# Batch 0's loads split by chunk and moved between queues, constant set-up moved to VectorE, and two early table-loading activations added, in a fused scan and MLP kernel

## The chip, the core and the metric

The kernel runs on one core of a Trainium2 chip. The core has five instruction streams that run side by side and wait for each other through semaphores: TensorE (PE, with its weight loads PEld shown apart), VectorE (DVE), ScalarE (ACT), GpSimd (POOL) and SyncE (SP). SP, ACT and POOL can also start DMA transfers; the time that such an instruction takes on its queue is shown as SPq, ACTq or POOLq. Each stream works through its instructions in the order in which they were built. The metric is the device time of one execution in microseconds (us); lower is better.

## What is computed

Two steps, one after the other. The first is a gated linear recurrence over 4 batches, 8 heads and 768 positions, with head size D = 32 and state size N = 16. The second is an MLP over the 3072 tokens that come out, with 256 model columns and 2048 hidden columns and a tanh-approximated GELU.

```python
# x: (4, 8, 768, 32), a: (4, 8, 768), B and C: (4, 8, 768, 16)
log_a = np.log(np.clip(a, 1e-06, 1.0))
for c in range(nc):                      # chunks of 32 positions in the reference
    cum = np.cumsum(la, axis=-1)
    L = np.exp(cum[:, :, :, None] - cum[:, :, None, :]) * causal
    M = np.einsum('bhin,bhjn->bhij', Cc, Bc) * L
    y_intra = np.einsum('bhij,bhjd->bhid', M, xc)
    y_inter = np.einsum('bhin,bhnd->bhid', Cc, state) * np.exp(cum)[:, :, :, None]
    y[:, :, sl] = y_intra + y_inter
    state = decay_full * state + (Bc, xc, decay_from_j summed over the chunk)
x2 = y.transpose(0, 2, 1, 3).reshape(3072, 256)
h = x2 @ w_in
g = 0.5 * h * (1 + tanh(sqrt(2 / pi) * (h + 0.044715 * h**3)))
out = g @ w_out                          # (3072, 256) float32
```

## The kernel before

The sequence is cut into chunks of Q = 128 positions, so NC = 6 chunks per batch and 24 in all. The eight heads are two groups (NG) of four (HPG); four heads of 32 rows each fill the 128 rows of TensorE.

**Prologue.** Two loads on SP bring the decays (`a_nat0`, `a_nat1`, lines 107 and 108). `emit_dma(0)` loads B and C of batch 0, each in two halves of four heads: B on SP (line 72), C on ACT's queue (line 76). GpSimd builds the constants: two identities, two triangular masks, a block mask, a column of ones, and zeros in the unused halves of the padded tiles (lines 110 to 131). TensorE transposes the decays (lines 134, 135), ACT takes logarithms (142, 143), one matmul sums them along the chunk (148), and ACT makes the scales `sclB` and `sclC` (151, 152) and the per-chunk decay `df2_sb` (171) with exponentials.

GpSimd then makes five decay matrices for the batch (`emit_dfm`, line 187: `dfm` for the chunks 1 to 5), multiplies B and C by their scales into the padded bf16 tiles (`emit_scales`, lines 210 and 216; four instructions of 128x384 for a batch, covering all six chunks of one head group each), and starts the loads of x with a cast to bf16 (`emit_x`, line 97, two halves) and of the MLP weights (lines 231 to 234).

**A chunk.** TensorE transposes four 128x128 pieces of scaled B and C (lines 283, 288; the tile is called `trans`), ACT copies them to SBUF (`bct_sb`, 294), eight small matmuls give the scores (329), DVE multiplies by the causal mask (`mtm`, 338), and TensorE forms the state update from x (351), the output inside the chunk (362) and the part from the state (371). DVE casts the output into `xt_all` (380) and updates the state `g` (387, 393). `g` of a chunk is needed by the next one, so chunks follow each other through DVE.

**The MLP.** As soon as 512 tokens (four chunks) exist, `emit_mlp_group` may run: 64 matmuls of 128x512 (249), 16 GELU activations (257), 64 matmuls of 128x256 (263), four copies by DVE (271) and four stores on SP (272). There are six such groups.

**What sets the order.** The code is traced into a graph, and a list scheduler decides the order of each engine's instructions from its own cost estimates. So an instruction can stand far from where the code writes it: loads and casts without inputs drift forward, and parts of a batch's chunks are interleaved with the MLP of earlier tokens. Loads on SP and ACT share eight completion counters in turn; from the ninth such load on, each waits, on its queue, for the landing of the load that used its counter last. The loads of batch 1's B and C are written inside batch 0's chunk loop, but the built program has them directly behind those of batch 0 on SP and on ACT.

## Time and profile before

| | before |
|---|---|
| time, median of 6 runs | 178.31 us (174.41 to 179.41) |
| time of the profiled execution | 177.68 us |
| its span | 175.9 us |
| PE busy | 142.1 us (81% of the span) |
| PEld busy | 80.7 us (46%) |
| ACT busy | 72.9 us (41%) |
| DVE busy | 60.4 us (34%) |
| POOL busy | 54.3 us (31%) |
| DMA packets | 80108, of which 74528 under 512 bytes |

All times in the text are counted from the start of the span. The profiled execution took 1.8 us more than its span, and lies 0.6 us under the median. PE is busy in 9 tenths or more of nearly every slice after about 36 us, and in 0 to 6 tenths ahead of that, so the run has two parts: a prologue and first chunks in which TensorE mostly waits, and a long part in which it is the busy engine. A row of the timeline gives the start, the duration, the engine, the line, the operation, output and inputs, and the number of instructions merged; in brackets stands the idle time ahead of it on its engine, with what ended it.

### The profile page before, as it was taken

The numbers are of one execution on the slowest core, as the hardware profiler recorded it, in microseconds if no ns is written. First come the engines' busy times: TensorE is split into PE (matmuls) and PEld (weight loads), VectorE is DVE, ScalarE is ACT, GpSimd is POOL, SyncE is SP. The second block draws the span as 40 slices with busy tenths as digits, with TensorE's granted clock in tenths as the row PEclk, the third lists the DMA queues.
The fourth block names the chain that finished last, engine by engine and source line by source line (L and its number), as shares of the span: only waits on it lengthen the run. The fifth ranks groups of instructions, "written<-read, shape, count | busy, mean of one in ns | idle before, by whom it ended". The sixth has DMA issues, their size and how long they took to land.

```text
span 175.9 us, 2803 instructions
## 1 busy us (share of the span) xinstructions
PE 142.1 (81%) x1156; PEld 80.7 (46%) x1156; DVE 60.4 (34%) x108; ACT 72.9 (41%) x128; POOL 54.3 (31%) x74
## 2 busy tenths in 40 slices
PE   1020536699999969999999995999999999999872
PEld 0010313334457624446746863334675444674561
DVE  0000117756024765501103566430356671110010
ACT  0070221164870325674386122248613568438400
POOL 8708999919997151470000000000000000000000
PEclk9999999999999975999999997559999999999999
DMA  7999299999999900099100110000001000010111
GB/s 84 118 92 112 20 134 196 197 110 39 41 71 125 94 4 2 0 36 85 63 30 28 35 60 0 4 0 0 30 31 62 0 0 4 33 57 30 34 41 48
DMA packets 80108, 9.45 MB, mean 54 GB/s; under 512 B 74528, under 2 KB 79840, under 8 KB 80096
## 3 DMA queue, kind: packets, MB, share of 16 engines
q0 software_dynamic: 51712, 4.46, 63.6%
q1 hardware_dynamic: 16032, 4.03, 12.3%
q10 hardware_dynamic: 12352, 0.79, 5.9%
q8 instruction: 9, 0.15, 0.3%
q14 instruction: 3, 0.02, 0.0%
HBM read 10.58 MB, written 3.15 MB: 78 GB/s over the span
## 4 chain that ended last, share of the span: by engine, by line
PE 72%; DVE 7%; ACTq 5%; ACT 5%; POOL 4%; DMA 3%; issue 2%
PE out_all L263 25%; ACTq L76 5%; PE ys_all L362 5%; PE ys_all L371 4%; PE mt_all L329 4%; DMA x_nat<-in_x_dram 3%; DVE mtm L338 3%; DVE o_sb L271 1%; DVE xt_all L380 1%; ACT gel L257 1%; PE ys_all L351 1%; ACT bct_sb L294 1%; PE trans L283 1%; POOL bs_pad_136 L210 1%; PE trans L288 1%
## 5 line engine op out<-in xcount | busy, mean ns | idle before, releaser
L263 PE MATMUL out_all<-w_181,gel 128*128 128x256 bf16 x384 | 57.2, 275 | 2.0 <-DVE o_sb L271 1.6
L263 PEld LDWEIGHTS <-gel 128*128 128x128 bf16 x384 | 37.4, 98 | 18.3 <-issue 3.5
L338 DVE TENSOR_TENSOR mtm<-mt_all,ut_mask 128x1024 bf16<-128x1024 f32 x24 | 29.2, 1215 | 21.5 <-PE mt_all L329 21.5
L294 ACT COPY bct_sb<-trans 128x512 bf16<-128x512 bf16 x24 | 13.6, 586 | 49.0 <-PE trans L288 33.3
L271 DVE COPY o_sb<-out_all 128x256 f32<-128x256 f32 x24 | 10.2, 425 | 63.3 <-PE out_all L263 63.3
L249 PEld LDWEIGHTS <-w_180 128*128 128x128 bf16 x192 | 18.7, 103 | 19.3 <-issue 9.9
L380 DVE CAST xt_all<-ys_all 128x256 bf16<-128x256 f32 x24 | 10.2, 424 | 27.7 <-PE ys_all L371 23.8
L362 PE MATMUL ys_all<-mtm,x_nat 128*32 128x128 bf16 x192 | 11.7, 249 | 2.8 <-DVE mtm L338 2.8
L362 PEld LDWEIGHTS <-x_nat 128*32 128x32 bf16 x192 | 5.1, 96 | 16.3 <-issue 14.4
L329 PE MATMUL mt_all<-bct_sb 16*128 16x128 bf16 x192 | 12.2, 247 | 0.6 <-ACT bct_sb L294 0.6
L97 POOL DMA_DIRECT2D x_nat<-in_x_dram x8 | 11.7, 1466 | 0.0
L371 PE MATMUL ys_all<-bct_sb,g 128*128 128x128 bf16 x40 | 10.1, 251 | 0.3 <-DVE g L393 0.3
L283 PE MATMUL trans<-ident_bf,bs_pad_136 128*128 128x128 bf16 x24 | 4.6, 261 | 5.2 <-POOL bs_pad_136 L210 4.7
L351 PE MATMUL ys_all<-x_nat,bs_pad_136 128*128 128x128 bf16 x24 | 4.5, 274 | 4.4 <-DMA x_nat<-in_x_dram 2.5
L329 PEld LDWEIGHTS <-bct_sb 16*128 16x128 bf16 x192 | 4.7, 95 | 5.5 <-issue 1.2
L148 PE MATMUL rcum_ps<-laT,sl_mask 128*128 128x192 f32 x2 | 1.0, 592 | 7.1 <-ACT laT L143 7.1
L87 POOL DMA_DIRECT2D c_nat<-in_C_dram x2 | 4.5, 2239 | 3.7 <-issue 3.7
L371 PEld LDWEIGHTS <-g 128*128 128x128 bf16 x40 | 3.9, 99 | 3.6 <-DVE g L393 0.4
L142 ACT ACT_TABLE_LOAD x1 | 1.3, 1283 | 9.9 <-issue 9.9
L288 PE MATMUL trans<-ident_bf,cs_pad_137 128*128 128x128 bf16 x24 | 4.7, 264 | 0.9 <-POOL cs_pad_137 L216 0.9
L283 PEld LDWEIGHTS <-bs_pad_136 128*128 128x128 bf16 x24 | 2.4, 113 | 5.8 <-POOL bs_pad_136 L210 5.2
L351 PEld LDWEIGHTS <-bs_pad_136 128*128 128x128 bf16 x24 | 2.9, 121 | 4.8 <-issue 4.5
(301 smaller groups left out, 209.8 us busy)
## 6 DMA issues: line engine op xcount, KB each, us to landing
out_dram<-o_sb SPq DMA_DIRECT2D x24, 128.0 KB, 1.7
x_nat<-in_x_dram POOLq DMA_DIRECT2D x8, 192.0 KB, 6.1
w_180<-in_moe_w_in_dram POOLq DMA_DIRECT2D x2, 512.0 KB, 8.0
w_181<-in_moe_w_out_dram POOLq DMA_DIRECT2D x2, 512.0 KB, 12.0
c_nat_105<-in_C_dram ACTq DMA_DIRECT2D x2, 192.0 KB, 5.6
b_nat_104<-in_B_dram SPq DMA_DIRECT2D x2, 192.0 KB, 6.4
c_nat_195<-in_C_dram ACTq DMA_DIRECT2D x2, 192.0 KB, 10.8
b_nat_194<-in_B_dram SPq DMA_DIRECT2D x2, 192.0 KB, 11.7
```

The source lines that it names most:

```text
L76: nc.scalar.dma_start(out=c_nat[:, dst].rearrange("p h c n -> p (h c) n"), in_=C[b, dst].rearrange("h (c q) n -> q (h c) n", q=Q),)
L97: nc.gpsimd.dma_start(out=x_nat[:, dst].rearrange("p h c d -> p (h c) d"), in_=x[b, dst].rearrange("h (c q) d -> q (h c) d", q=Q),)
L249: nc.tensor.matmul(out=h1_ps[i], lhsT=w1[:, half, ft * 128 : (ft + 1) * 128], rhs=xt_all[:, half, tok0 : tok0 + TG], start=(half == 0), st ...
L263: nc.tensor.matmul(out=o_ps, lhsT=gel[:, kt, tt * 128 : (tt + 1) * 128], rhs=w2[:, kt, :], start=(kt == 0), stop=(kt == NFT - 1),)
L271: nc.vector.tensor_copy(out=o_sb, in_=o_ps)
L294: nc.scalar.copy(out=bct_sb, in_=trans_ps)
L329: nc.tensor.matmul(out=mt_all[:, k, g, c % 2, :], lhsT=bct_sb[32 * k : 32 * k + N, 2 * g, :], rhs=bct_sb[32 * k : 32 * k + N, 2 * g + 1, : ...
L338: nc.vector.tensor_tensor(out=mtm, in0=mt_all[:, :, :, c % 2, :], in1=ut_b, op=ALU.mult)
L351: nc.tensor.matmul(out=ys_all[:, 1, g], lhsT=bs_pad[:, c, h0 : h0 + HPG].rearrange("p h n -> p (h n)"), rhs=x_nat[:, h0 : h0 + HPG, c, :], ...
L362: nc.tensor.matmul(out=ys_all[32 * k : 32 * (k + 1), 0, g], lhsT=x_nat[:, h0 + k, c, :], rhs=mtm[:, k, g, :], start=True, stop=(c == 0), t ...
L371: nc.tensor.matmul(out=ys_all[:, 0, g], lhsT=g_all[:, g, :], rhs=csTs[g], start=False, stop=True,)
L380: nc.vector.tensor_copy(out=xt_all[:, :, tok0 : tok0 + Q], in_=ys_all[:, 0, :, :])
```

## The change

Seven edits:

1. Batch 0's B, C and x are loaded chunk by chunk (six chunks of 128 positions, all eight heads) in fp32. SP gets B of all chunks, C of the first two and x of all (14 loads); ACT's queue gets C of the chunks 2 to 5. Batch 1 still uses the half-batch loads, the batches 2 and 3 still come by POOL.
2. x of batch 0 is no longer cast by POOL's load; it lands as `x0f` and GpSimd casts each chunk into `x_nat0` with an instruction of its own (new line 270).
3. The scaling of batch 0 is done chunk by chunk (`emit_scale_chunk0`, new lines 264 and 267: 128x128 each, twelve in all) and written around `emit_dfm(0)` and the weight loads.
4. Some constants move from GpSimd to DVE: the zeros of the padded tiles, the ones, and the bf16 identity, which becomes a cast of the fp32 one.
5. A tiny exponential at the very start (new line 106) and a tiny GELU after `df2_sb` (new line 199) are added on ACT.
6. Every second store of an MLP group goes to ACT's queue (new line 326).
7. The order of the mask set-up on GpSimd changes.

```diff
@@ -64,7 +64,7 @@
     out_all = pp_out.tile([128, 2, DM], FP32, name="out_all")
 
     def emit_dma(b):
-        if b <= 1:
+        if b == 1:
             b_nat = singles.tile([128, NH, NC, N], FP32, name=f"b_nat{b}")
             c_nat = singles.tile([128, NH, NC, N], FP32, name=f"c_nat{b}")
             for h0 in (0, HPG):
@@ -100,34 +100,55 @@
             )
         return x_nat
 
+
+    warm = singles.tile([128, 4], FP32)
+    nc.vector.memset(warm, 1.0)
+    nc.scalar.activation(out=warm, in_=warm, func=AF.Exp)
+
     a_v = a.rearrange("b h (c q) -> (b h c) q", q=Q)
     NBHC = NB * NH * NC
     a_nat0 = singles.tile([128, 128], FP32)
     a_nat1 = singles.tile([128, 128], FP32)
     nc.sync.dma_start(out=a_nat0, in_=a_v[0:128, :])
     nc.sync.dma_start(out=a_nat1[0 : NBHC - 128, :], in_=a_v[128:NBHC, :])
-    tiles0 = emit_dma(0)
+
+    b_nat0 = singles.tile([128, NC, NH, N], FP32)
+    c_nat0 = singles.tile([128, NC, NH, N], FP32)
+    x0f = singles.tile([128, NC, NH, D], FP32)
+    for c in range(NC):
+        sl = slice(c * Q, (c + 1) * Q)
+        nc.sync.dma_start(
+            out=b_nat0[:, c], in_=B[0, :, sl, :].rearrange("h q n -> q h n")
+        )
+        if c < 2:
+            nc.sync.dma_start(
+                out=c_nat0[:, c], in_=C[0, :, sl, :].rearrange("h q n -> q h n")
+            )
+        nc.sync.dma_start(
+            out=x0f[:, c], in_=x[0, :, sl, :].rearrange("h q d -> q h d")
+        )
+
     ident_f32 = singles.tile([128, 128], FP32)
     make_identity(nc, ident_f32)
-    ident_bf = singles.tile([128, 128], BF16)
-    make_identity(nc, ident_bf)
     sl_mask = singles.tile([128, 128], FP32)
     make_lower_triangular(nc, sl_mask, val=1.0, diag=False)
-    ut_mask = singles.tile([128, 128], BF16)
-    make_upper_triangular(nc, ut_mask, val=1.0, diag=True)
-    ones32 = singles.tile([128, 32], FP32)
-    nc.gpsimd.memset(ones32, 1.0)
     maskblk = singles.tile([128, 128], BF16)
     nc.gpsimd.memset(maskblk, 0.0)
     for k in range(HPG):
         nc.gpsimd.memset(maskblk[32 * k : 32 * k + N, 32 * k : 32 * (k + 1)], 1.0)
-
+    ut_mask = singles.tile([128, 128], BF16)
+    make_upper_triangular(nc, ut_mask, val=1.0, diag=True)
+
+    ident_bf = singles.tile([128, 128], BF16)
+    nc.vector.tensor_copy(out=ident_bf, in_=ident_f32)
+    ones32 = singles.tile([128, 32], FP32)
+    nc.vector.memset(ones32, 1.0)
     pads = {}
     for sl in range(2):
         bs = pad_pool.tile([128, NC, NH, 32], BF16, name=f"bs_pad{sl}")
         cs = pad_pool.tile([128, NC, NH, 32], BF16, name=f"cs_pad{sl}")
-        nc.gpsimd.memset(bs[:, :, :, N:32], 0.0)
-        nc.gpsimd.memset(cs[:, :, :, N:32], 0.0)
+        nc.vector.memset(bs[:, :, :, N:32], 0.0)
+        nc.vector.memset(cs[:, :, :, N:32], 0.0)
         pads[sl] = (bs, cs)
 
     aT_ps = pp_big.tile([128, 2, 128], FP32, tag="big", padded_shape=[128, 2, 256])
@@ -151,6 +172,12 @@
     nc.scalar.activation(out=sclB, in_=rcum_ps, func=AF.Exp)
     nc.scalar.activation(out=sclC, in_=rcum_ps, func=AF.Exp, scale=-1.0)
 
+    for c in range(2, NC):
+        sl = slice(c * Q, (c + 1) * Q)
+        nc.scalar.dma_start(
+            out=c_nat0[:, c], in_=C[0, :, sl, :].rearrange("h q n -> q h n")
+        )
+
     NDC = NB * NG * NC
     df2_ps = pp_big.tile([128, NDC], FP32, tag="big", padded_shape=[128, TG])
     for k in range(HPG):
@@ -169,6 +196,7 @@
         )
     df2_sb = singles.tile([128, NDC], FP32)
     nc.scalar.activation(out=df2_sb, in_=df2_ps, func=AF.Exp)
+    nc.scalar.activation(out=warm, in_=warm, func=AF.Gelu_apprx_tanh)
 
     def emit_dfm(b):
         dfms = [None]
@@ -221,17 +249,42 @@
             )
         return bs_pad, cs_pad
 
-    dfms = emit_dfm(0)
-    loaded = emit_scales(0, tiles0)
-    x_nat0 = emit_x(0)
+    x_nat0 = singles.tile([128, NH, NC, D], BF16)
+
+    def emit_scale_chunk0(c):
+        bs_pad, cs_pad = pads[0]
+
+        def scl_ap(t):
+            return bass.AP(
+                tensor=t.tensor,
+                offset=t.offset + c,
+                ap=[t.ap[0], [NC, NH], [0, N]],
+            )
+
+        nc.gpsimd.tensor_tensor(
+            out=bs_pad[:, c, :, 0:N], in0=b_nat0[:, c], in1=scl_ap(sclB), op=ALU.mult
+        )
+        nc.gpsimd.tensor_tensor(
+            out=cs_pad[:, c, :, 0:N], in0=c_nat0[:, c], in1=scl_ap(sclC), op=ALU.mult
+        )
+        nc.gpsimd.tensor_copy(out=x_nat0[:, :, c, :], in_=x0f[:, c])
 
     w1 = singles.tile([128, 2, DF_], BF16)
     w2 = singles.tile([128, NFT, DM], BF16)
     w2_v = moe_w_out.rearrange("(kt p) dm -> p kt dm", p=128)
+
+    emit_scale_chunk0(0)
+    emit_scale_chunk0(1)
+    dfms = emit_dfm(0)
+    emit_scale_chunk0(2)
     nc.gpsimd.dma_start(out=w1[:, 0, :], in_=moe_w_in[0:128, :])
+    emit_scale_chunk0(3)
     nc.gpsimd.dma_start(out=w1[:, 1, :], in_=moe_w_in[128:256, :])
+    emit_scale_chunk0(4)
     nc.gpsimd.dma_start(out=w2[:, 0:8, :], in_=w2_v[:, 0:8, :])
+    emit_scale_chunk0(5)
     nc.gpsimd.dma_start(out=w2[:, 8:NFT, :], in_=w2_v[:, 8:NFT, :])
+    loaded = pads[0]
 
     xt_all = singles.tile([128, NG, NTOK], BF16)
 
@@ -269,7 +322,8 @@
                 )
             o_sb = osb_pool.tile([128, DM], FP32, name="o_sb")
             nc.vector.tensor_copy(out=o_sb, in_=o_ps)
-            nc.sync.dma_start(
+            eng = nc.sync if tt % 2 == 0 else nc.scalar
+            eng.dma_start(
                 out=out[tok0 + tt * 128 : tok0 + (tt + 1) * 128, :], in_=o_sb
             )
 
```

The scheduler has the last word on where these stand. Three places in the built program follow.

ACT's stream from its start to the scales. `c_nat_105` and `c_nat_195` are C of batch 0 and batch 1 before, `c_nat_108` and `c_nat_223` the same in the change; `laT` is the logarithm of the decays. Before:

```order
L76 DMA c_nat_105<-in_C_dram 128x24x16 x2
L76 DMA c_nat_195<-in_C_dram 128x24x16 x2
L142 ACT_TABLE_LOAD
L142 ACTIVATE laT<-aT_ps 128x128
L143 ACTIVATE laT<-aT_ps 128x64
L151 ACT_TABLE_LOAD
L151 ACTIVATE sclB<-rcum_ps 128x192
```

And in the change:

```order
L177 DMA c_nat_108<-in_C_dram 128x8x16
L106 ACT_TABLE_LOAD
L106 ACTIVATE warm<-warm 128x4
L177 DMA c_nat_108<-in_C_dram 128x8x16 x3
L199 ACT_TABLE_LOAD
L199 ACTIVATE warm<-warm 128x4
L76 DMA c_nat_223<-in_C_dram 128x24x16 x2
L163 ACT_TABLE_LOAD
L163 ACTIVATE laT<-aT_ps 128x128
L164 ACTIVATE laT<-aT_ps 128x64
L172 ACT_TABLE_LOAD
L172 ACTIVATE sclB<-rcum_ps 128x192
```

The tiny GELU has moved ahead of the logarithm, the two tables that the tiny activations load are both replaced again before any large activation uses them, and the loads of batch 1's C still stand ahead of the logarithm. Further on, the table load in front of the first large GELU (line 257 before, 310 now) is there in both programs.

GpSimd's stream from the end of the set-up to the first scaled chunk. `w_180` are the MLP's first weights, `bs_pad` and `cs_pad` the padded, scaled B and C of batch 0. Before:

```order
L97 DMA x_nat<-in_x_dram 128x24x32
L187 TENSOR_TENSOR dfm_163<-maskblk,df_sb 128x256
L187 TENSOR_TENSOR dfm_165<-maskblk,df_sb 128x256
L187 TENSOR_TENSOR dfm_167<-maskblk,df_sb 128x256
L187 TENSOR_TENSOR dfm_169<-maskblk,df_sb 128x256
L187 TENSOR_TENSOR dfm_171<-maskblk,df_sb 128x256
L210 TENSOR_TENSOR bs_pad_136<-b_nat_104,sclB 128x6x4x16
L216 TENSOR_TENSOR cs_pad_137<-c_nat_105,sclC 128x6x4x16
```

And in the change:

```order
L270 CAST x_nat_179<-x0f 128x8x32 x3
L280 DMA w_180<-in_moe_w_in_dram 128x2048
L270 CAST x_nat_179<-x0f 128x8x32
L282 DMA w_180<-in_moe_w_in_dram 128x2048
L264 TENSOR_TENSOR bs_pad_147<-b_nat_107,sclB 128x8x16
L267 TENSOR_TENSOR cs_pad_148<-c_nat_108,sclC 128x8x16
```

The casts of x for the chunks 0 to 3 have moved ahead of every scaling, so the first scaling now stands behind the landing of x's fourth chunk. Two chunks are scaled ahead of the five `dfm`, the chunks 2 to 4 behind them, chunk 5 after the first load of the second weights.

TensorE's stream at the end of batch 0's third chunk. `bs_pad_140` and `bs_pad_151` are the scaled B of batch 1, `cs_pad_141` and `cs_pad_152` its scaled C; `bs_pad_136` and `bs_pad_147` belong to batch 0. Before:

```order
L351 LDWEIGHTS bs_pad_136
L351 MATMUL ys_all<-x_nat,bs_pad_136 128x128
L283 LDWEIGHTS bs_pad_140
L283 MATMUL trans<-ident_bf,bs_pad_140 128x128
L288 LDWEIGHTS cs_pad_141
L288 MATMUL trans<-ident_bf,cs_pad_141 128x128
```

And in the change (a pair of transposes of the other head group stands right ahead of these rows):

```order
L337 LDWEIGHTS bs_pad_151
L337 MATMUL trans<-ident_bf,bs_pad_151 128x128
L342 LDWEIGHTS cs_pad_152
L342 MATMUL trans<-ident_bf,cs_pad_152 128x128
L405 LDWEIGHTS bs_pad_147
L405 MATMUL ys_all<-x_nat_179,bs_pad_147 128x128
```

All four transposes of batch 1's first chunk now stand ahead of the fourth chunk's state matmuls, where three of them followed those matmuls before, and the fourth came later still. In both programs the twelve transposes of the chunks 2 to 4 of batch 0 stand ahead of the first chunk's output matmuls. From the first MLP group on, TensorE's order is nearly the same in both.

## The prediction

> **What bounds the kernel now.** I read the slices of the page first: PE is mostly idle up to about 36 us and busy afterwards. The change touches the idle part and the stores, so the question is what starts TensorE's long part, and the chain of waits and the timeline answer it. First the start, from the timeline: the C loads on ACT's queue, the first logarithm's table, the first decay matrix and the first scaling on GpSimd.
>
> ```profile
> 3.18 6.72 ACTq L76 DMA_DIRECT2D c_nat_195<-in_C_dram  x2
> ...
> 4.27 0.36 PE L135 MATMUL aT_ps<-ident_f_110,a_nat_101 64*128 64x64 f32 x1 [1.09 <-DMA a_nat_101<-in_a_dram]
> ...
> 9.93 1.28 ACT L142 ACT_TABLE_LOAD   x1 [9.93 <-issue]
> 11.22 0.28 ACT L142 ACTIVATE laT<-aT_ps 128x128 f32<-128x128 f32 x1
> ...
> 12.93 0.33 ACT L151 ACTIVATE sclB<-rcum_ps 128x192 f32<-128x192 f32 x1
> ...
> 13.67 0.61 POOL L187 TENSOR_TENSOR dfm_163<-maskblk,df_sb 128x256 bf16<-128x256 bf16 x1 [6.12 <-ACT df_sb L171]
> ```
>
> ACT did nothing but start loads until 9.9 us, and the two loads for batch 1 took 6.72 us of that. The decays had been transposed by 4.63. GpSimd then waited 6.12 us for ACT and began at 13.67. The chain of waits carries on through GpSimd to the load of x:
>
> ```profile
> 14.28 0.57 POOL dfm_165 L187
> ...
> 16.57 0.83 POOL bs_pad_136 L210
> ...
> 19.86 6.03 DMA x_nat<-in_x_dram
> ...
> 26.58 0.42 DVE xt_all L380
> ...
> 29.53 0.42 DVE xt_all L380
> ...
> 32.69 0.42 DVE xt_all L380
> ```
>
> The second half of x stands behind the scaling in GpSimd's stream, starts at 19.86 and lands 6.03 us later, and only then does the first chunk's output appear (26.58). Chunks follow at about 3.1 us. The same timeline, further on, gives what GpSimd did for batch 1 and when TensorE left for the MLP:
>
> ```profile
> 22.40 0.92 POOL L233 DMA_DIRECT2D w_181<-in_moe_w_out_dram  x1
> ...
> 24.15 2.87 POOL L97 DMA_DIRECT2D x_nat<-in_x_dram  x2
> ...
> 26.97 0.94 POOL L210 TENSOR_TENSOR bs_pad_140<-b_nat_194,sclB 128x384 bf16<-128x384 f32 x1
> ...
> 29.47 0.92 POOL L216 TENSOR_TENSOR cs_pad_141<-c_nat_195,sclC 128x384 bf16<-128x384 f32 x1
> ...
> 33.50 0.37 PE L351 MATMUL ys_all<-x_nat,bs_pad_136 128*128 128x128 bf16 x2 [0.62 <-DVE t_301 L387]
> ...
> 34.63 0.30 PE L362 MATMUL ys_all<-mtm,x_nat 128*32 128x128 bf16 x4 [0.44 <-DVE mtm L338]
> ...
> 36.42 1.01 PE L249 MATMUL h_414<-xt_all,w_180 128*128 128x512 bf16 x2
> ```
>
> Batch 1 was scaled by 30.39 (29.47 + 0.92); TensorE asked for it after 33.50, so GpSimd had some 3 us to spare. The MLP began at 36.42. Two stretches of the windows view, one at the MLP's start and one in its middle, show how little idle time TensorE has from there on:
>
> ```profile
> 36.00:50.00 14.00, 13.82 (x81) 5.95 (x77) 5.36 (x9) 9.84 (x16) 10.58 (x10) 1.00 3.78 61
> 80.00:100.00 20.00, 19.82 (x158) 13.06 (x157) 4.44 (x10) 9.59 (x17) 0.00 (x0) 1.00 0.32 49
> ```
>
> The number behind the comma is PE's busy time: 13.82 of 14 us and 19.82 of 20. So the change is worth what it moves the MLP's start (36.42), and no more unless the later part alters.
>
> **What the change removes, and what is late next.** It removes the wait for x by POOL (x now comes by SP), and lets the first chunk go when its own pieces are there. But the built order puts new things in the way, and two streams decide when GpSimd can start scaling, a time that I call s: the data of x's fourth chunk, and ACT's scales.
>
> *The data.* Ahead of the first scaling GpSimd casts four chunks of x and starts the two loads of the first weights. x's fourth chunk is the tenth of SP's chunk loads. The windows view gives the rate for such small pieces while only SP and ACT load (last number: GB/s), and the rate once POOL's casting load of x joins:
>
> ```profile
> 0.00:4.00 4.00, 0.45 (x1) 0.18 (x1) 0.00 (x0) 0.00 (x0) 3.20 (x20) 1.00 0.65 78
> 4.00:5.00 1.00, 0.36 (x1) 0.18 (x1) 0.00 (x0) 0.00 (x0) 1.00 (x2) 1.00 1.45 137
> 11.00:12.00 1.00, 0.24 (x1) 0.27 (x2) 0.00 (x0) 0.97 (x4) 0.00 (x0) 1.00 1.93 79
> ```
>
> A chunk of B or C is 65.5 KB, one of x 131 KB, the decays 98 KB. Up to x's fourth chunk that is 10 x 65.5 + 4 x 131 + 98 = 1277 KB; 78 x 4 = 312 KB of it goes in the first 4 us, the other 965 KB at 137 GB/s take 7.0: 11.1 us. x's pieces are twice as long; if a piece costs the same whatever its length, x counts half, 1015 KB, and it is 9.1. Batch 1's C (393 KB on ACT's queue) can slip in and cost up to 2.9: 13.9. Between 9.1 and 13.9 I take 11.5. A cast of 256 elements is not in the trace; the two-input `dfm` of that size took 0.57, so 0.3 to 0.57, and I take 0.4. The issue of a load of the first weights (and a row for later, the table load at the first large GELU):
>
> ```profile
> 21.87 0.56 POOL L232 DMA_DIRECT2D w_180<-in_moe_w_in_dram  x1
> ...
> 37.05 1.28 ACT L257 ACT_TABLE_LOAD   x1
> ```
>
> That makes 11.5 + 0.4 + 0.56 = 12.5 by the data.
>
> *ACT.* Its stream now holds four small C loads, two table loads with tiny activations, batch 1's two C loads, and then the logarithm. The issues of the C loads before, from the chain of waits:
>
> ```profile
> 0.80 0.46 ACTq L76
> 1.29 1.86 ACTq L76
> 3.18 3.12 ACTq L76
> 6.34 3.55 ACTq L76
> ```
>
> An issue takes 0.46 on an empty queue and up to 3.55 behind others. The four small loads at 0.46 are 1.84, two table loads 2.56, two tiny activations at an estimated 0.2 each (`laT` with 128 elements takes 0.28): 0.8 + 1.84 + 2.56 + 0.4 = 5.6. Batch 1's two C loads cost 0.46 to 3.55 each, and with less queued ahead than before I take the 1.86: 9.3 for the logarithm's table, against 9.93 (bounds 6.5 and 12.7). From there to the end of `sclB` took 13.26 - 9.93 = 3.33, so ACT is ready at 12.7 (bounds 9.9 and 16.0). So ACT, too, ends up about where it was; the two early activations cost it 3 us and save nothing, because the built order reloads both tables, and the table load at 37.05 stays (1.28 us, which would have been their gain).
>
> The Trainium skill speaks against these edits more strongly: *ScalarE: Activation LUTs*, "What ACT_TABLE_LOAD costs", puts a switch at 1283 ns for the load plus about 1380 ns of draining. The trace agrees with the load and not with the drain: loaded at 9.93 for 1.28, and `laT` runs at 11.22. By the page ACT would be ready 2.8 us later still, at about 15.5, and the sum below would come out 2.3 us longer, near 175; that is the late start among the rivals.
>
> Two uncertain times, 12.5 and 12.7, of which the later counts: s = 13.2.
>
> *GpSimd from s.* Twelve scalings of 128 elements: 0.57 for 256 and 0.83 for 384 lie on a line that gives 0.31 for 128, so 3.7 (bounds 3.3, the four old instructions together, and 6.8, at 0.57 each). Five `dfm`: 2.9. Two casts: 0.8. Two loads of the second weights: 1.8. Batch 1's x: 2.87. Batch 1's scaling, 26.97 to 30.39: 3.4. Together 15.5, so batch 1 is scaled at 28.7. That is 1.7 us earlier than before, and now it matters, because TensorE comes earlier.
>
> *TensorE.* In its order the first chunk's output stands behind the transposes of the chunks 2 to 4, which need ten scalings and the `dfm`: s + 6.0 = 19.2. Output matmuls and cast add about 1.1, of which the cast is 0.42: first output at 20.3, third at 26.6 (two steps of 3.16), and 0.8 later, at 27.4, TensorE reaches batch 1's transposes (before, 33.50 - 32.69). GpSimd is ready at 28.7: a wait of 1.3 us. The last transposes and the two state matmuls then take some 0.6 (the state matmuls 0.37 before). The mask product of that chunk has long been made, so the output matmuls start at 29.3 (34.63 before). From there to the MLP took 36.42 - 34.63 = 1.79: 31.1. The gain is 5.3 us.
>
> *The rest at nothing.* Two rows of the page and one of the stores' answer:
>
> ```profile
> L338 DVE TENSOR_TENSOR mtm<-mt_all,ut_mask 128x1024 bf16<-128x1024 f32 x24 | 29.2, 1215 | 21.5 <-PE mt_all L329 21.5
> ...
> b_nat_194<-in_B_dram SPq DMA_DIRECT2D x2, 192.0 KB, 11.7
> ```
>
> ```profile
> L272 SPq DMA_DIRECT2D out_dram<-o_sb x24: 332/332/354, 52.0 to 172.9; - x24
> ```
>
> DVE's new memsets and cast run while it is idle: it sat idle for its first 21.5 us. ACT's twelve stores cost 0.33 us of issue each, as SP's did; they stand where the first store's copy is due anyway, and ACT is busy for 41% of the span. If that cover is gone, each costs 0.33, 4.0 in all. The first weights start some 9 us earlier and are needed at 31; the second start at 20 to 23, as before.
>
> So: 177.68 - 5.3 = 172.4 in terms of the profiled execution, which lies 0.6 under the median of 178.31; for a median I say 173.0.
>
> **The rivals.** *The clock decides more than the prologue.* In these rows of the windows view the third number from the end is the granted clock:
>
> ```profile
> 64.00:68.00 4.00, 3.53 (x25) 1.30 (x24) 1.92 (x5) 1.78 (x3) 0.61 (x1) 0.50 0.00 0
> 68.00:72.00 4.00, 4.00 (x29) 1.83 (x28) 1.53 (x3) 1.79 (x3) 0.61 (x1) 0.68 0.01 2
> 142.00:150.00 8.00, 7.89 (x62) 3.71 (x61) 2.86 (x6) 5.64 (x10) 0.00 (x0) 1.00 0.01 2
> ```
>
> The dip at 64 to 72 cost 4 x 0.50 + 4 x 0.32 = 3.3 us; batch 3 has the same work at 142 to 150 with no dip. The change shifts the work by 5 us, so a dip may go (169.7) or one more may come (176.3). For it: the six runs before spread over 5 us. Against: nothing in the later order changes much. The Trainium skill, *TensorE: Matmul & The Clock Gate*, Part 1, has the clock decided in free-running windows of about 3.4 us; by that rule either can happen by chance. The trace agrees that the same work can run at 0.50 and at 1.00.
>
> *GpSimd starts late.* ACT needs its upper bound of 16.0 (two issues of 3.55, or table loads that hold it longer than 1.28), or the loads share with batch 1's and land late: s between 15 and 17, batch 1 scaled at 31 to 32.5, gain 1.5 to 3.5, time 175 to 177. The second half of batch 1's B works the same way: the page has 11.7 us from issue to landing, and it now stands behind sixteen loads.
>
> *Slower.* The casts in front of the scaling hold GpSimd until x's fourth chunk is there. At the 79 GB/s of the row at 11.00 the same data, with batch 1's C, take 4 + (1277 + 393 - 312) / 79 = 21.2 us; s = 22.2, batch 1 is scaled at 37.7, and TensorE gets it 4.2 us later than the 33.5 at which it asked: some 182. It decides from s = 18.0 on, where 18.0 + 15.5 = 33.5. Against: that rate was seen only beside POOL's casting load, and that one is gone here.
>
> **Chances.** The forecast 0.58; a dip gone 0.12, one more 0.08; GpSimd late 0.15; slower 0.07. The range takes in the bounds of s (11 to 15.5, gains of 7.5 to 3), a dip either way and most of the late case: 169.5 to 177.2. This kernel can tell about 2%, 3.6 us, so faster means under 174.7. The forecast falls there in five cases of six (0.48), the lost dip always: 0.60. The other sixth, the added dip and the late start are no change: 0.33. Slower: 0.07.
>
> **What would show it.** Right: five table loads on ACT, the last still ahead of the first large GELU; GpSimd's first scaling at 12 to 15 us behind a wait for x or for ACT; the first output near 20; TensorE waiting for GpSimd ahead of batch 1's first transposes near 28; the MLP starting near 31; an unchanged length from there to the end. Wrong: a first scaling after 18, a first output under 17, TensorE not waiting there, or a later part that differs by more than 2 us at the same clock.

## The result, and the profile after

The changed kernel took 180.89 us in the median (178.64 to 182.66, 10 runs) against 177.82 for the kernel before in the same comparison (174.41 to 179.41, 20 runs); the ratio is 1.023 with a 95% interval of 1.014 to 1.032. It is slower, by about 3 us, where 5.3 were to be gained; the interval leaves open whether by more than 2%. Medians here are of all executions, ratios leave out those that ran in a slower state of the chip. Its profiled execution took 180.24 us with a span of 178.5; before it was 177.68 and 175.9.

The timeline of the changed kernel, its start and the MLP's beginning:

```profile
8.86 0.40 POOL L270 CAST x_nat_179<-x0f 128x256 bf16<-128x256 f32 x1 [5.95 <-DMA x0f<-in_x_dram]
...
10.91 0.38 ACTq L76 DMA_DIRECT2D c_nat_223<-in_C_dram  x1
11.31 1.28 ACT L163 ACT_TABLE_LOAD   x1 [6.08 <-DMA b_nat_107<-in_B_dram]
...
13.02 1.28 ACT L172 ACT_TABLE_LOAD   x1
14.31 0.33 ACT L172 ACTIVATE sclB<-rcum_ps 128x192 f32<-128x192 f32 x1
...
19.12 0.39 POOL L270 CAST x_nat_179<-x0f 128x256 bf16<-128x256 f32 x1 [1.40 <-DMA x0f<-in_x_dram]
19.45 0.55 POOL L282 DMA_DIRECT2D w_180<-in_moe_w_in_dram  x1
20.02 0.42 POOL L264 TENSOR_TENSOR bs_pad_147<-b_nat_107,sclB 128x128 bf16<-128x128 f32 x1
...
34.64 0.86 POOL L238 TENSOR_TENSOR bs_pad_151<-b_nat_222,sclB 128x384 bf16<-128x384 f32 x1
...
35.47 0.86 POOL L244 TENSOR_TENSOR cs_pad_152<-c_nat_223,sclC 128x384 bf16<-128x384 f32 x1
...
36.40 0.29 PE L342 MATMUL trans<-ident_bf,cs_pad_152 128*128 128x128 bf16 x1 [0.54 <-POOL cs_pad_152 L244]
...
38.63 0.59 PE L302 MATMUL h_442<-xt_all,w_180 128*128 128x512 bf16 x1 [0.38 <-DVE xt_all L434]
38.72 1.28 ACT L310 ACT_TABLE_LOAD   x1
```

GpSimd waits for x chunk by chunk (the profile's page puts these waits at 14.4 us), casts the fourth chunk at 19.12 and makes its first scaling at 20.02, 5.4 us after ScalarE had the scales (14.64). From there it runs without a gap to 36.33, TensorE waits for it, and the MLP starts at 38.63, 2.2 us later than before (36.42). From the MLP's start to the end it is 178.5 - 38.63 = 139.9 us, before 139.5. So the loss lies ahead of the MLP.

The windows of the same kernel (last number: GB/s), and one source line's answer, that of batch 1's two B loads:

```profile
0.00:4.00 4.00, 0.81 (x2) 0.36 (x2) 1.72 (x7) 1.76 (x3) 2.09 (x15) 1.00 0.52 65
4.00:10.00 6.00, 0.00 (x0) 0.00 (x0) 0.00 (x0) 1.22 (x2) 0.40 (x1) 1.00 1.70 109
10.00:16.00 6.00, 1.30 (x10) 0.71 (x10) 0.00 (x0) 3.61 (x7) 0.40 (x1) 1.00 1.72 104
...
4.00:19.00 15.00, 1.30 (x10) 0.71 (x10) 0.00 (x0) 4.83 (x9) 1.83 (x4) 1.00 1.67 108
...
L72 SPq DMA_DIRECT2D b_nat_222<-in_B_dram x2: 3953/4172/4392, 18.7 to 23.1; - x2
DMA to landing us min/median/max: 8.8/9.3/9.8
```

From 4 to 16 us the transfers run at 104 to 109 GB/s, from 4 to 19 at 108. And batch 1's second B load, issued at 23.1, lands at 31.9 to 32.9: GpSimd asked for it at 34.64, so a front that is 1.7 to 2.7 us earlier meets it.

### The profile page after: what moved, and what is told of

Same layout as the page of the kernel before. It is cut to its first block, busy times and chain, and to the rows that moved or that the text cites. A ratio compares the mean times of both kernels' runs of the same rounds, so it can differ in the third digit from the quotient of the medians.

```text
span 178.5 us, 2832 instructions
## 1 busy us (share of the span) xinstructions
PE 142.5 (80%) x1156; PEld 79.8 (45%) x1156; DVE 62.8 (35%) x115; ACT 76.0 (43%) x132; POOL 51.6 (29%) x79
## 3 DMA queue, kind: packets, MB, share of 16 engines
q0 software_dynamic: 45536, 4.06, 75.7%
q1 hardware_dynamic: 22688, 3.38, 15.5%
## 4 chain that ended last, share of the span: by engine, by line
PE 68%; POOL 10%; SPq 5%; ACT 4%; DVE 4%; DMA 3%; issue 3%; ACTq 0%; POOLq 0%
PE out_all L316 24%; PE ys_all L416 4%; PE ys_all L425 4%; DMA x0f<-in_x_dram 3%; PE mt_all L383 3%; ACT gel L310 3%; SPq L120 2%; DVE o_sb L324 2%; POOL x_nat L97 2%; ACT bct_sb L348 2%; SPq L127 1%; PE ys_all L405 1%; POOL bs_pad_147 L264 1%; DVE mtm L392 1%; POOL cs_pad_148 L267 1%
## 5 line engine op out<-in xcount | busy, mean ns | idle before, releaser
L302 PEld LDWEIGHTS <-w_180 128*128 128x128 bf16 x192 | 18.6, 102 | 19.0 <-issue 9.5
L337 PE MATMUL trans<-ident_bf,bs_pad_147 128*128 128x128 bf16 x24 | 5.5, 259 | 9.4 <-POOL bs_pad_147 L264 8.9
L97 POOL DMA_DIRECT2D x_nat<-in_x_dram x6 | 8.6, 1430 | 2.4 <-issue 2.4
L416 PE MATMUL ys_all<-mtm,x_nat 128*32 128x128 bf16 x144 | 8.5, 240 | 1.0 <-DVE mtm L392 0.9
L416 PEld LDWEIGHTS <-x_nat 128*32 128x32 bf16 x144 | 3.7, 95 | 9.6 <-issue 8.0
L337 PEld LDWEIGHTS <-bs_pad_147 128*128 128x128 bf16 x24 | 2.5, 104 | 10.0 <-POOL bs_pad_147 L264 9.6
L270 POOL CAST x_nat_179<-x0f 128x256 bf16<-128x256 f32 x6 | 2.4, 395 | 14.4 <-DMA x0f<-in_x_dram 14.4
L342 PE MATMUL trans<-ident_bf,cs_pad_148 128*128 128x128 bf16 x24 | 5.1, 259 | 0.3
L337 PE MATMUL trans<-ident_bf,bs_pad_151 128*128 128x128 bf16 x24 | 4.4, 226 | 1.1 <-POOL bs_pad_151 L238 0.5
L342 PE MATMUL trans<-ident_bf,cs_pad_152 128*128 128x128 bf16 x24 | 4.2, 225 | 0.9 <-POOL cs_pad_152 L244 0.9
L169 PEld LDWEIGHTS rcum_ps<-laT,sl_mask 128*128 128x128 f32 x2 | 0.5, 313 | 9.4 <-issue 9.4
```

What stands on the lines that cost most here:

```text
L97: nc.gpsimd.dma_start(out=x_nat[:, dst].rearrange("p h c d -> p (h c) d"), in_=x[b, dst].rearrange("h (c q) d -> q (h c) d", q=Q),)
L302: nc.tensor.matmul(out=h1_ps[i], lhsT=w1[:, half, ft * 128 : (ft + 1) * 128], rhs=xt_all[:, half, tok0 : tok0 + TG], start=(half == 0), st ...
L337: nc.tensor.transpose(out=trans_ps[:, 2 * g, :], in_=bs_pad[:, c, h0 : h0 + HPG].rearrange("p h n -> p (h n)"), identity=ident_bf,)
L342: nc.tensor.transpose(out=trans_ps[:, 2 * g + 1, :], in_=cs_pad[:, c, h0 : h0 + HPG].rearrange("p h n -> p (h n)"), identity=ident_bf,)
L416: nc.tensor.matmul(out=ys_all[32 * k : 32 * (k + 1), 0, g], lhsT=x_nat[:, h0 + k, c, :], rhs=mtm[:, k, g, :], start=True, stop=(c == 0), t ...
```

## The experiments

Each ratio is to the kernel before, run beside it. Lines of traces are from timelines unless the text says another view.

**The casts' place alone.** With `tc.issue_after` each cast is tied behind the scalings of its chunk, on the same engine and with the same loads; `last` is the second scaling of the chunk. The rest of the edit, not shown, ties the weights and batch 1's x behind casts, in the places that the code gives them. So w1, whose issues stood among the casts ahead of the first scaling in the changed kernel as built (17.03 and 19.45), now stands behind the scalings of the chunks 2 and 3 (20.84 and 22.68).

```diff
-        nc.gpsimd.tensor_copy(out=x_nat0[:, :, c, :], in_=x0f[:, c])
+        with tc.issue_after(last.ins):
+            cast = nc.gpsimd.tensor_copy(out=x_nat0[:, :, c, :], in_=x0f[:, c])
```

> The changed kernel with one thing moved in GpSimd's order: each cast of x stands behind the scalings of its chunk instead of four of them ahead of all scalings; weights, x of batch 1 and all loads keep their places in the lists, on the same queues. Theory 1 (the casts cost the front, but batch 1's second B load, which landed at about 32 in the changed kernel, 2 us before GpSimd asked for it at 34.64, comes next): the first scaling starts at about 14.6 with the scales instead of 20.02, GpSimd then waits for x's chunks one by one and for batch 1's B, the MLP starts at 36 to 38 instead of 38.63 and the time falls by 1 to 2.5 us, to 178 to 179.5. Theory 2 (the casts' place is the whole loss): everything behind the first scaling comes 5.4 us earlier, the MLP starts at 33.2 and the time is 175 or less. Theory 3 (the weights, issued earlier too, push batch 1's B out by as much as the front gains): the MLP starts at 38.5 or later and the time does not fall.

176.64 us, ratio 0.995 (0.990 to 1.000): 4.3 us under the changed kernel.

```profile
14.73 0.78 POOL L264 TENSOR_TENSOR bs_pad<-b_nat,sclB 128x128 bf16<-128x128 f32 x2 [11.83 <-ACT sclB L172]
...
32.35 0.63 PE L308 MATMUL h<-xt_all,w 128*128 128x512 bf16 x1
...
35.20 0.88 POOL L238 TENSOR_TENSOR bs_pad<-b_nat,sclB 128x384 bf16<-128x384 f32 x1 [3.27 <-DMA b_nat<-in_B_dram]
...
36.13 0.29 PE L343 MATMUL trans<-ident_bf,bs_pad 128*128 128x128 bf16 x1 [2.62 <-POOL bs_pad L238]
...
38.53 0.61 PE L308 MATMUL h<-xt_all,w 128*128 128x512 bf16 x1
```

The first scaling comes with the scales, 5.3 us earlier, and then batch 1's second B load is late by 3.27 us, as the first theory had it. Its time of 178 to 179.5 was missed low. In the order built here TensorE makes one matmul of the MLP (32.35) ahead of batch 1's transposes, waits 2.62 us for the scaling, and goes on with the MLP at 38.53, about where the changed kernel starts it (38.63); but the fifth chunk's output is cast at 38.41 by then, in the changed kernel at 41.86. So the place of the casts, with w1's two issues among them, is the changed kernel's loss; what the other order on TensorE adds was not separated. Without that loss the change is worth about nothing.

**Casts on VectorE.** `nc.gpsimd.tensor_copy` became `nc.vector.tensor_copy`.

> The changed kernel with the six casts of x on VectorE, so that GpSimd no longer waits for x ahead of its first scaling. Theory 1 (the casts in front of the scalings are what delays): the first scaling starts when ScalarE's table is ready, about 14.6 us (20.02 in the changed kernel); GpSimd then has batch 1 scaled about 30 to 31 (36.3), and the MLP starts about 34 (38.63), so the time falls by 4 to 5 us against the changed kernel, to some 176. Theory 2 (the late landing of the loads is what delays, whoever waits for it): the first scaling comes at 14.6 too, but the B chunks 4 to 6, x's chunks and batch 1's second B load, which land late on SyncE's queue (the last about 27), hold TensorE and GpSimd one after another, and the time falls by less than 2 us, to 179 or more.

181.1 us, ratio 1.017 (1.007 to 1.027). The first scaling came later than either theory had it:

```profile
3.53 0.55 POOL L282 DMA_DIRECT2D w<-in_moe_w_in_dram  x1
...
15.41 1.28 ACT L163 ACT_TABLE_LOAD   x1 [9.91 <-DMA b_nat<-in_B_dram]
...
18.82 0.41 POOL L264 TENSOR_TENSOR bs_pad<-b_nat,sclB 128x128 bf16<-128x128 f32 x1 [14.74 <-DMA b_nat<-in_B_dram]
```

With the casts gone the scheduler issued the first weights at once. Their megabyte went ahead of the small loads, ScalarE's issue of batch 1's C waited until 15 for an earlier load, and the logarithm behind it. So the run says nothing on the casts; it showed that ScalarE is held by transfers.

**Fewer loads.** Batch 0's x in two loads of four heads.

> The changed kernel with batch 0's x in two fp32 loads of four heads, where it was six loads of a chunk: the same bytes and the same 128-byte pieces on the same queue, in four loads fewer. Theory 1 (loads wait for the landing of earlier ones, through the eight counters that they share, and the queue runs empty): the pieces now flow as in the kernel before, at about 137 GB/s, and x has landed by 13 us. Theory 2 (one queue moves small pieces at about 20 ns each per DMA engine, whatever the waits): the 12,288 pieces up to the end of x's second load take 15 to 16 us from about 3, and x lands at 18 to 20. The time itself says little here, since every chunk's y needs both x loads; by theory 1 it is 3 us or more under the changed kernel, by theory 2 within 2 us of it.

186.57 us, ratio 1.049 (1.042 to 1.056). The second load of x was cast at 25.34; both theories expected it earlier. Fewer loads did not help, but the run cannot tell whether their number was a limit: the built order had again put the weights first (issued at 2.84 and 3.53), so x shared the engines with them.

**x on a third queue.** The six x loads on GpSimd's queue.

> The changed kernel with the six fp32 loads of x issued on GpSimd's queue (after the identity and the first mask) where they were on SyncE's: the same loads, pieces and casts. Theory 1 (SyncE's queue alone was too slow for 14 of 18 loads): two queues side by side move over 140 GB/s between 4 and 10 us, x's fourth chunk and batch 0's last B chunk have landed by about 13, the first scaling starts with ScalarE's table, 12 to 14.6, the MLP starts 33 to 34, and the time is 4 to 6 us under the changed kernel. Theory 2 (the 16 DMA engines together gave no more than 105 to 110 GB/s for such pieces): the batch-0 loads are through at about 18 as before, the window shows 110 GB/s or less, and the time is within 2 us of the changed kernel.

181.23 us, ratio 1.018 (1.010 to 1.026). In the windows:

```profile
4.00:12.00 8.00, 0.10 (x1) 0.00 (x0) 0.00 (x0) 1.28 (x2) 4.13 (x11) 1.00 1.28 136
12.00:16.00 4.00, 0.00 (x0) 0.00 (x0) 0.00 (x0) 0.00 (x0) 0.00 (x0) 1.00 1.27 76
```

136 GB/s at first, between the two theories, then 76. The time was set elsewhere: batch 1's C was issued at 14.56 to 17.30 on ScalarE's queue, the table loaded at 17.34, and the first scaling came at 20.75, behind the scales. x, whose last load was issued at 6.2 and took at most 8.0 us, was there in time; that was not enough.

**No early activations.** Both tiny activations left out; the output does not use them.

> The changed kernel without the two early activations on a small tile (and so without the two table loads in front of them); the output does not use them. Theory 1 (the first scaling waits for x, not for ScalarE): ScalarE is ready up to 3 us earlier than 14.6, the first scaling still starts at about 20.0, and the time is within 1 us of the changed kernel. Theory 2 (the early activations cost time on the path): the time falls by about 3 us.

179.42 us, ratio 1.012 (1.005 to 1.020). The logarithm's table is loaded at 8.51 instead of 11.31, the first scaling is at 20.26 and the MLP at 38.66 where they were. The trace is as the first theory had it; the medians differ by 1.5 us, half a microsecond more than it allowed, and the intervals overlap.

**Side edits alone.** The kernel before with the early activations, the memsets and identity on VectorE and every second store on ScalarE.

> The kernel before with the side edits alone: the two early activations, the memsets and the bf16 identity on VectorE, every second store on ScalarE's queue; batch 0's loads and scalings stay as in the kernel before. In the order that it is built with, GpSimd now issues both halves of x and the first half of w1 ahead of everything else. Theory 1 (the side edits by themselves lie beside other work): the time is within 1.5 us of the kernel before, 176 to 179. Theory 2 (the edits cost: the first activations hold ScalarE, or the stores disturb the MLP): 2 us or more above it, and the stretch from the MLP's start to the end is longer than 139.5 us by as much. Theory 3 (the early x takes away the wait for x in front of the first output): 2 to 3 us under it.

179.78 us, ratio 1.014 (1.008 to 1.019), between the first two theories. GpSimd, with fewer memsets, issued x and half of w1 by 6.3 us; the table came at 13.73 and the MLP at 37.23 (0.8 later). From there to the end 140.3 (0.8 longer). The early x did not pay. The changed kernel does not lose by these edits: the run with the casts behind the scalings holds them all, at 0.995.

**Batch 1's C out of the way.** On SyncE's queue behind batch 0's loads, in the changed kernel and in the kernel before. The edit in the changed kernel, where this line loads batch 1 alone (in the kernel before it picks the queue by the batch):

```diff
-                nc.scalar.dma_start(
+                nc.sync.dma_start(
                     out=c_nat[:, dst].rearrange("p h c n -> p (h c) n"),
```

> The changed kernel with batch 1's two C loads on SyncE's queue, behind its other loads, where they were on ScalarE's queue ahead of Ln and among batch 0's loads. Theory 1 (ScalarE stood behind those two issues, and the 16 DMA engines together give some 105 to 110 GB/s for such small pieces whichever queue they come from): ScalarE's Ln table is loaded at about 5.5 and its scales are ready at 9 instead of 14.6; SyncE's queue alone still moves 100 to 110 GB/s between 10 and 16 us; 1.28 MB lie ahead of the end of x's fourth chunk instead of 1.67, so that it lands at about 14 (18.9 in the changed kernel) and the first scaling starts at 14.5 to 15; the MLP starts about 33.5 and the time is about 175, 5 us under the changed kernel. Theory 2 (one queue by itself is limited to 20 ns per piece and DMA engine): 10,240 pieces on SyncE's queue take 13 us, the rate falls to about 76 GB/s once ScalarE's four C loads are through, the fourth chunk lands at 16 to 17, and the time is 177 to 178.

186.25 us, ratio 1.040 (1.032 to 1.048). First a window, then the timeline:

```profile
9.00:14.00 5.00, 0.00 (x0) 0.00 (x0) 0.00 (x0) 0.00 (x0) 1.74 (x4) 1.00 1.24 127
```

```profile
5.24 1.28 ACT L163 ACT_TABLE_LOAD   x1
...
15.50 0.42 POOL L264 TENSOR_TENSOR bs_pad<-b_nat,sclB 128x128 bf16<-128x128 f32 x1
...
35.25 0.87 POOL L238 TENSOR_TENSOR bs_pad<-b_nat,sclB 128x384 bf16<-128x384 f32 x1 [5.33 <-DMA b_nat<-in_B_dram]
40.48 0.87 POOL L244 TENSOR_TENSOR cs_pad<-c_nat,sclC 128x384 bf16<-128x384 f32 x1 [4.36 <-DMA c_nat<-in_C_dram]
```

The front went nearly as the first theory said: table at 5.24, first scaling 4.5 us earlier, half a microsecond behind its range. SyncE's queue by itself moved 127 GB/s, so a limit of one queue is not what held two at 104 to 109. The Trainium skill, *DMA: Bandwidth & Descriptors*, "Issuing engines are not separate DMA queues", says that all issuers share the same 16 engines; the rows fit that, though the mix of pieces differs. But batch 1's last B and C loads now landed at 35 and 40 us, and the time is 8 us above what the worse theory gave.

> The kernel before with one edit: batch 1's two C loads on SyncE's queue in place of ScalarE's. Theory 1 (its Ln waited for ScalarE's third and fourth load issue, until 9.93): the Ln table is loaded at about 3.5, the scales are ready at 7, GpSimd's four scalings end about 13.5 instead of 19.9, x's second half is issued then, the first output comes at 21 to 22 instead of 26.6, the MLP starts at 31 to 32 instead of 36.4, and the time falls by 4 to 5 us, to about 173. Theory 2 (the loads' landing is what sets the MLP's start): x's second half and batch 1's B and C now land together, the MLP starts at 34 to 35 and the time falls by 2 us or less.

174.56 us, ratio 0.983 (0.976 to 0.990), between the theories. The table is loaded at 3.22, the first output is 5.7 us earlier (20.91), and then the same follows: GpSimd's last batch-1 scaling waits 9.40 us, until 32.87, for the second C load.

**C behind the last Exp**, on ScalarE's own queue:

```diff
-                    tiles_next = emit_dma(b + 1)
+                    with tc.issue_after(df_exp.ins):
+                        tiles_next = emit_dma(b + 1)
```

> The changed kernel with one thing moved: batch 1's two C loads stay on ScalarE's queue but are issued behind its last Exp of the decays instead of ahead of Ln. Theory 1 (what the changed kernel lost is the order of transfers: batch 1's C among batch 0's loads, with Ln held behind their issue): the scales are ready at 9 instead of 14.6; x's fourth chunk lands at 14.5 to 17, the first scaling starts at 15 to 17.5 instead of 20.02, batch 1's C has landed before GpSimd asks for it, the MLP starts 18.6 after the first scaling as in the changed kernel, 34 to 36, and the time is 175.5 to 177.5. Theory 2 (whatever is taken from the front comes back at batch 1's loads, behind the weights that GpSimd now issues earlier, as in the run with those loads on SyncE's queue, 186): GpSimd waits for batch 1's B or C after 28, the MLP starts at 38 or later, and the time is 180 or more.

182.97 us, ratio 1.030 (1.025 to 1.036): theory 2. The first scaling is at 15.63, within the first theory's range, and the MLP starts at 41.58, 3 us later than in the changed kernel:

```profile
15.63 0.42 POOL L264 TENSOR_TENSOR bs_pad<-b_nat,sclB 128x128 bf16<-128x128 f32 x1
...
37.59 0.87 POOL L238 TENSOR_TENSOR bs_pad<-b_nat,sclB 128x384 bf16<-128x384 f32 x1 [6.61 <-DMA b_nat<-in_B_dram]
```

**Also the casts on VectorE, and w2 late.** (A version of it with C on SyncE's queue and w2 in its old place gave 1.030, 1.021 to 1.039; its profiled execution took 631 us and is not read.)

> The changed kernel with the order of its transfers mended at three places: batch 1's C behind the last Exp on ScalarE's queue, the casts of x on VectorE, w1 behind the scalings as in the changed kernel's list and w2 behind batch 1's scaling. Theory 1 (the 16 DMA engines move some 105 GB/s of these small pieces, so that what lands first is what counts): the first scaling starts at 9 to 10, VectorE's first mask step follows x's sixth chunk at about 17, the outputs come from 19 on, 3 us apart, batch 1 is scaled by 26 to 28 without a long wait, the MLP starts at 29.5 to 31 and the time is 171 to 173. Theory 2 (the loading of small chunks itself costs, by counters shared between queues or by the number of loads): batch 1's loads still come late, the MLP starts at 34 or later and the time is 176 or more.

180.7 us, ratio 1.018 (1.013 to 1.022): theory 2. The first scaling comes at 8.87, 11 us earlier than in the changed kernel, and the MLP at 39.22:

```profile
8.87 0.41 POOL L266 TENSOR_TENSOR bs_pad<-b_nat,sclB 128x128 bf16<-128x128 f32 x1 [5.96 <-ACT sclB L172]
...
35.08 1.02 POOL L240 TENSOR_TENSOR bs_pad<-b_nat,sclB 128x384 bf16<-128x384 f32 x1 [3.42 <-DMA b_nat<-in_B_dram]
```

**Then the weights and batch 1's x as well behind batch 1's scaling:**

> The same as the run with the casts on VectorE and batch 1's C behind the last Exp (180.7, batch 1's second B load landed at 35.1), with one thing moved: w1, w2 and batch 1's x are all issued behind batch 1's scaling on GpSimd. Theory 1 (a load of small pieces that is in flight beside the weights' large pieces gets hardly any of the 16 engines until these are through): with no weights in flight, all of batch 0 has landed by 17 to 18 and batch 1's B and C by 23 to 26, at 90 to 110 GB/s; the first output comes at 19 to 20, batch 1 is scaled by 26, w1 lands at 31 to 32, the MLP starts about then and the time is 172 to 175. Theory 2 (batch 1's B comes late for its place behind 16 loads on SyncE's queue and their shared counters, weights or not): its second half lands at 30 or later, the MLP starts after 36, since w1 now comes behind it, and the time is 177 or more.

178.91 us, ratio 1.003 (0.997 to 1.009). The windows and the answer for the B loads' line, first without this move, then with it:

```profile
20.00:24.00 4.00, 2.33 (x31) 1.54 (x30) 2.97 (x4) 0.00 (x0) 1.14 (x1) 1.00 1.14 209
24.00:30.00 6.00, 1.22 (x16) 0.56 (x15) 2.22 (x4) 0.59 (x1) 0.06 (x1) 1.00 1.76 90
...
DMA to landing us min/median/max: 15.4/17.6/19.7
```

```profile
20.00:24.00 4.00, 2.17 (x31) 1.50 (x30) 3.19 (x5) 0.00 (x0) 0.99 (x2) 1.00 1.75 98
24.00:30.00 6.00, 1.71 (x21) 0.66 (x17) 2.63 (x4) 0.58 (x1) 4.80 (x8) 1.00 0.20 11
...
DMA to landing us min/median/max: 8.5/9.7/10.9
```

With GpSimd's loads in flight the engines move 209 GB/s from 20 to 24 and batch 1's B takes 15 to 20 us; without them 98 and 8.5 to 10.9, and B lands by 26.2 instead of 35.1. For the landing of B that is theory 1: it was not the place behind 16 loads. The time is above its range, because w1 now starts at 30.61 and the MLP, started at 36.22, still waits 1.62 us for it at 39.09. Which of w1 and batch 1's x takes how much was not separated.

**The kernel before with two things moved**, batch 1's C behind the last Exp and w2 behind batch 1's scaling:

> The kernel before, batch 0 loaded whole, with two things moved: batch 1's C loads on ScalarE's queue behind its last Exp instead of ahead of Ln, and w2's two loads behind batch 1's scaling. Theory 1 (order of transfers): the scales are ready at 7, batch 0 is scaled at about 13.8, the first output comes at 21, batch 1's second C load lands by 21 to 23 (it was 32 with both on SyncE's queue), batch 1 is scaled at about 23 to 25 and the MLP starts at 30.5 to 31.5; the time is 171.5 to 173, and it beats the kernel before by 5 to 6 us without any load per chunk. Theory 2 (batch 1's loads come late in whichever queue they stand, because x and w1 on GpSimd's queue take the engines): the MLP starts at 33 to 34 as with them on SyncE's queue, and the time is 174 to 175.

173.42 us, ratio 0.967 (0.957 to 0.976), between the theories. It beats both kernels, without a load per chunk.

```profile
21.50 0.27 PE L356 MATMUL ys_all<-x_nat,bs_pad 128*128 128x128 bf16 x1 [1.50 <-DMA x_nat<-in_x_dram]
...
21.76 0.88 POOL L218 TENSOR_TENSOR cs_pad<-c_nat,sclC 128x384 bf16<-128x384 f32 x1
...
32.16 1.01 PE L249 MATMUL h<-xt_all,w 128*128 128x512 bf16 x2 [0.38 <-DVE xt_all L385]
```

Batch 1 is scaled by 22.64 without a wait, and the MLP starts 4.3 us earlier than in the kernel before; the medians lie 4.2 apart. (The profiled execution took 170.39 us, 3 under the median: the clock dip at 64 to 72 is not in it, where 1.00 was granted, and 0.59 in the kernel before.) Two attempts to go on from it failed.

> The same as the run beside it, with the memsets of the padded tiles on VectorE and both halves of x issued on GpSimd's queue at once, from about 3 us, and w1 and batch 1's x behind batch 0's scalings. Theory 1 (x's second half was what the first output waited for): batch 0's B and C land 3 us later for it, its scaling ends at 15 to 16, the first output comes at 17.5 to 19, batch 1 is scaled at 24 to 26, the MLP starts at 27.5 to 29.5 and the time is 169 to 171. Theory 2 (the sum of the bytes decides, not their order): everything batch 0 needs lands at 17 to 19, batch 1's loads at 25 to 27 with w1 between them, the MLP starts at 30.5 to 32 and the time is 172 to 173, as beside it.

178.94 us, ratio 1.012 (1.004 to 1.019). The first output came at 22.73, no earlier: TensorE waited 4.06 us, until 19.10, for x, which now shared the engines with all of B and C. And batch 1's second B load, still in flight when w1 was issued at 15.36, was scaled at 30.33 after a wait of 7.86. It is slower than either theory.

> The kernel before, batch 0 loaded whole, with its transfers in the order in which they are needed: both halves of x at once on GpSimd's queue (memsets of the padded tiles on VectorE), w1 behind batch 0's scaling, batch 1's B and C on ScalarE's queue behind the first copy of the transposed tiles, w2 and batch 1's x behind batch 1's scaling. Theory 1 (only one stream at a time need be in flight): batch 0's B, C and x land by 12 to 13, batch 0 is scaled by 13.5, the first output comes at 16 to 18, w1 lands by 21, batch 1's B and C behind it by 26 to 29, the MLP starts at 28.5 to 30.5 and the time is 169.5 to 172. Theory 2 (whatever comes last of the 4 MB of batch 0, w1, batch 1's B and C sets the MLP's start, in any order that keeps the engines busy): the MLP starts at 31.5 to 33 as in the best version so far, and the time is 172.5 to 174.5.

179.39 us, ratio 1.006 (1.000 to 1.011); the profiled execution was 1.8 us above that. The first output came at 18.28, near the forecast, and then

```profile
15.80 8.15 ACTq L76 DMA_DIRECT2D c_nat<-in_C_dram  x1
...
27.51 1.07 ACT L297 COPY bct_sb<-trans 128x512 bf16<-128x512 bf16 x2 [11.54 <-issue]
```

ScalarE's issue of batch 1's C took 8.15 us beside w1, and its copies for the later chunks stood behind it: second output at 31.34. Neither theory had a cost for the issuing engine.

## Why the prediction was wrong

The rival called *Slower* came true: the casts in front of the scaling held GpSimd until x's fourth chunk was there, and it decided, as it said, from s = 18.0 on; s was 20.02. Its rule (20.02 + 15.5 - 33.5 = 2.0 us lost) gives 179.7 for the profiled execution, which took 180.24. Its own figure, some 182, came from 79 GB/s, a rate that did not occur (104 to 109). It had 7% of the chance.

**The step that failed is the data term of s:** 12.5 predicted, 20.0 measured, because x's fourth chunk landed at about 19 and not at 11.5. By the windows 65 GB/s x 4 us (the trace's first 4 us) and 108 x 15 make 1.88 MB by 19 us. The 1277 KB that I counted, at this rate, are there at 4 + (1277 - 260) / 108 = 13.4; the rate of 137, taken from a single microsecond, was worth 2.3 us against the 11.1 of the working. The other 5.5 us are some 600 KB that I counted small or not at all. Of these, 393 are batch 1's C, for which I allowed up to 2.9 us and took next to nothing. The fifth chunks of B and x (197), in flight beside the fourth, would make up the rest; the first weight load, issued at 17.03, may have a part, and no view splits it. With C out of the way the first scaling came 4.5 us earlier (15.50), in a run whose rate was higher too (127 from 9 to 14). Whether the waits of loads for earlier landings slowed the queue as well stays open.

**ACT's term** was 12.7 and measured 14.64, within its bounds. The cause was another than the length of the issues: the second C load's issue stood until 10.91, waiting for the landing of a B load of SyncE's queue. That the early activations cost ScalarE some 3 us and save nothing held (the logarithm's table at 8.51 without them, at 11.31 with them; five table loads, the last at 38.72 ahead of the first large GELU).

**GpSimd from s:** 16.3 against 15.5, as a scaling of 128 elements comes every 0.37 and not 0.31 (twelve: 0.7). **TensorE:** s + 18.6 to the MLP against s + 17.9, with the predicted wait ahead of batch 1's transposes. Both held. **The later part** is unchanged within 0.4 us and the stores on ScalarE cost nothing that shows. The clock dips at 64 to 72 and 108 to 116 are in both profiles.

**The second mistake was hidden by the first.** "The first weights start some 9 us earlier" was costed at nothing. Had s been 13.2, batch 1's second B load would have been the next wait: at s = 14.73 GpSimd waited for it until 35.20, and in two runs that also move other loads until 37.59 (s = 15.63) and 35.08 (s = 8.87). The late rival named that load and left 1.5 to 3.5 us of gain; in the run at 14.73 it was 0.75, with an interval that reaches down to nothing. So the forecast of 5.3 us looks out of reach with this list of transfers, whatever the casts do; no run has s at 13.2 itself.

## What to carry to other kernels

Where a prologue is made of small pieces, add up the bytes that stand ahead of the one awaited, from every queue, and use the rate of a long window; then do the same for the next load awaited, since a faster front issues the large loads sooner and these push it back. Look in the built order for an instruction that waits for data ahead of work that is ready: moving the casts behind the scalings was worth 4.3 us. Keep load issues off an engine that has work on the path until that work is issued.

## What the hardware showed unexpectedly

- SyncE's queue by itself moved its mix of 64- and 128-byte pieces at 127 GB/s, two queues with more of the 64-byte ones 104 to 109, and with GpSimd's loads in flight it was 209. Beside these, small loads took 15.4 to 19.7 us to land instead of 8.5 to 10.9.
- Issuing a load can hold its engine: for 8.15 us on ScalarE beside w1, and for 6.08 until a load of another engine's queue had landed.
- A table load takes 1.28 us and the next activation runs at once (13.02, then 14.31). The Trainium skill, *ScalarE: Activation LUTs*, "What ACT_TABLE_LOAD costs", adds a drain of about 1.4 us; no load here shows it.
